# Strassen's product for all three up-projections of a maxout layer, with scan steps and output products placed between its halves

## Chip, cores and metric

One core of a Trainium2 chip. The metric is the device time of one execution in microseconds (us), as the median of several executions. TensorE does the matmuls, VectorE (DVE) and ScalarE (ACT) the work on their results, GpSimd (POOL) helps, SyncE (SP) issues transfers.

## The reference, cut to what matters

A chunked scan (Mamba-2) over 4 sequences of 768 tokens gives x of shape 3072 x 256. A feed-forward layer of the kind "maximum of three" follows, all in fp32:

```python
h = np.maximum(np.maximum(x @ w1, x @ w2), x @ w3)   # 256 -> 768, three times
return (h @ w_out).astype(np.float32)                # 768 -> 256
```

The kernels work on six blocks of 512 tokens. While TensorE does the products of block c, the scan of block c+1 goes on in pieces: transposes (trB, trC), scores (s), state (A) and outputs (y).

## The kernel before

It uses Strassen's product (seven products of half size for eight, in the variant with fewer sums) for w1 alone, from block two on. w2 and w3 go by plain products of 512 columns. A round for two of the six column tiles of w1 has four early products, three VectorE sums that hang on each other, and three late products that add to the same PSUM banks:

```python
def early(c, q):
    A, B = (ps.tile([P, 2, HB], FP32, tag=tag, bufs=1, name=tag) for tag in SUMS)
    quarter_sums(c, q, [(1, A, 0), (6, A, 1), (5, B, 0), (7, B, 1)], True)
    ...
    nc.scalar.copy(out=eu[:, 0], in_=A[:, 0])
    nc.vector.tensor_tensor(out=eu[:, 1], in0=A[:, 1], in1=eu[:, 0], op=ALU.add)
    nc.vector.tensor_tensor(out=v[:, 0], in0=B[:, 1], in1=eu[:, 1], op=ALU.add)
    nc.vector.tensor_tensor(out=parts[:, 3], in0=B[:, 0], in1=v[:, 0], op=ALU.add)

def late(c, q):
    ...
    quarter_sums(c, q, [(2, A, 0), (3, B, 0), (4, B, 1)], False)
```

Between early and late lie long plain products, and the scan steps come with their VectorE work at once:

```python
def scores(n, b):
    scan_weights(n, b, scan_scores(n, b))        # 8 small matmuls, then 4 products on VectorE
...
for q in range(NQ):
    m = late(c, q)
    if n < NC:
        (lambda: transposed(n), lambda: scores(n, 0), lambda: scores(n, 2))[q]()
    ...
    for i in range(1, 3):
        for g in range(2):
            if i == 2 and g == 1 and q + 1 < NQ:
                early(c, q + 1)
            p = group(c, i, 2 * q + g)           # plain product, 512 columns
            ...                                  # running maximum on VectorE
```

At the end of block one stand, in VectorE's order: the last score weights, the state, four sums of w1's quarters, and only then the last step that decodes the third part of wo (`sign()`).

## Time and profile before

| | before |
|---|---|
| median time, us | 319.42 |
| span of the profiled run, us | 318.6 |
| TensorE busy | 94% |
| VectorE busy | 47% |
| length of a steady block, us | 47.3 |
| TensorE idle at the scores, all six blocks, us | 2.9 |

The prediction below shows the engine shares, the clock row, a steady block and the end of block one. This group is what the case turns on; it is the scores' line in the table of the costliest groups (line, engine, operation, count, busy us, mean ns, then TensorE's idle time just before these instructions and what ended it):

```profile
L467 PE MATMUL s<-CT,BT 32*128 32x256 f32 x192 | 14.9, 399 | 2.9 <-ACT CT L417 2.9
```

TensorE hardly waits here, and only twice, for ScalarE's CT before block two (1.36 and 1.55 us).

### The profile page before, as it was taken

Reading aid. Unit: us, or ns where it says so; the run is one execution under the profiler, and the core shown is the slowest. Engines: PE = TensorE matmul, PEld = TensorE weight load, DVE = VectorE, ACT = ScalarE, POOL = GpSimd, SP = SyncE. Lnnn points to the kernel's source line nnn. Section 1 sums busy time; section 2 is a strip of 40 time slices with the busy share of each in tenths; the row PEclk is TensorE's granted clock in tenths of the full one; section 3 lists DMA queues with packets and bytes.
Section 4 is the critical chain, followed back from the end, with each engine's and each line's share of the span. In section 5 each row is a group of like instructions: output and inputs, shape, how many; then the busy total and the mean of one; then the engine's idle time right before and its main releaser. Section 6 shows DMA issues by size and latency. Waiting matters only on the chain.

```text
span 318.6 us, 4707 instructions
## 1 busy us (share of the span) xinstructions
PE 300.0 (94%) x1836; PEld 193.1 (61%) x1836; DVE 150.9 (47%) x268; ACT 108.3 (34%) x281; POOL 55.3 (17%) x58
## 2 busy tenths in 40 slices
PE   6879998659999999999999999999999999999995
PEld 4633443347866548865548865648865658855574
DVE  2597773990336560346460347560347551344410
ACT  2857369510465050460150560241560002100000
POOL 5134563572000600000700000600000000000000
PEclk9999999976999999999999999999999999999999
DMA  7995999891069900077900088701000001000001
GB/s 88 240 387 168 186 249 164 203 120 21 29 189 175 99 0 27 9 209 149 107 2 33 2 232 142 89 0 35 0 34 3 0 0 35 30 5 0 0 0 66
DMA packets 105014, 28.09 MB, mean 88 GB/s; under 512 B 75296, under 2 KB 101920, under 8 KB 104992
## 3 DMA queue, kind: packets, MB, share of 16 engines
q1 hardware_dynamic: 104688, 27.66, 42.1%
q8 instruction: 14, 0.23, 0.3%
q10 hardware_dynamic: 304, 0.13, 0.1%
q14 instruction: 8, 0.07, 0.1%
HBM read 24.54 MB, written 3.24 MB: 87 GB/s over the span
## 4 chain that ended last, share of the span: by engine, by line
PE 80%; DVE 8%; ACT 5%; POOL 2%; issue 2%; DMA 1%; ACTq 0%; POOLq 0%; DVEq 0%
PE up L533 35%; PE o L621 20%; PE sumB L586 8%; PE sumA L586 6%; PE y L497 3%; PE s L467 3%; ACT L L387 2%; DVE L L476 2%; PE y L489 2%; DVE w_u L173 1%; PE spread L313 1%; ACT w_u L172 1%; POOL w_u L182 1%; POOL L L376 1%; DVE w L185 1%
## 5 line engine op out<-in xcount | busy, mean ns | idle before, releaser
L533 PE MATMUL up<-yT,w 128*128 128x512 f32 x312 | 141.0, 597 | 1.5 <-DVE w L185 1.5
L533 PEld LDWEIGHTS up<-yT,w 128*128 128x128 f32 x312 | 57.5, 190 | 65.7 <-issue 57.1
L621 PE MATMUL o<-wo,h 128*128 128x256 f32 x288 | 69.5, 397 | 3.7 <-DVE wo L185 3.7
L621 PEld LDWEIGHTS o<-wo,h 128*128 128x128 f32 x288 | 56.9, 200 | 15.6 <-DVE wo L185 4.1
L387 ACT ACTIVATE L<-L,ncums 128x128 f32<-128x128 f32 x160 | 49.7, 393 | 12.8 <-POOL L L376 12.8
L627 ACT COPY ob<-o 128x512 f32<-128x512 f32 x12 | 7.0, 585 | 77.4 <-PE o L621 77.4
L747 DVE TENSOR_TENSOR h<-m,up 128x512 f32<-128x512 f32 x30 | 20.6, 688 | 26.5 <-PE up L533 26.5
L476 DVE TENSOR_TENSOR L<-s,L 128x512 f32<-128x512 f32 x48 | 29.7, 683 | 3.5 <-PE s L467 3.5
L747 DVE TENSOR_TENSOR m<-m,up 128x512 f32<-128x512 f32 x30 | 20.5, 685 | 21.9 <-PE up L533 21.9
L601 ACT COPY halves<-sumA 128x256 f32<-128x256 f32 x15 | 5.6, 372 | 61.3 <-PE sumA L586 61.3
L511 DVE TENSOR_TENSOR rb<-y,yT 128x256 f32<-128x256 f32 x10 | 4.2, 420 | 41.4 <-ACT yT L502 41.4
L182 POOL TENSOR_TENSOR w_u<-w_u,w_r 128x512 uint32<-128x512 uint32 x12 | 18.1, 1507 | 31.2 <-DVE w_u L176 27.2
L376 POOL TENSOR_SCALAR_AFFINE_SELECT L<-L 128x1024 f32<-128x1024 f32 x20 | 22.8, 1167 | 0.0
L611 DVE TENSOR_TENSOR m<-sumB,halves 128x512 f32<-128x512 f32 x15 | 10.4, 692 | 20.5 <-PE sumB L586 20.5
L586 PE MATMUL sumA<-yT,w 128*128 128x256 f32 x60 | 17.8, 379 | 0.0
L467 PE MATMUL s<-CT,BT 32*128 32x256 f32 x192 | 14.9, 399 | 2.9 <-ACT CT L417 2.9
L586 PEld LDWEIGHTS sumA<-yT,w 128*128 128x128 f32 x60 | 11.4, 190 | 10.1 <-issue 7.2
L453 POOL TENSOR_TENSOR old<-S,E 128x256 f32<-128x256 f32 x4 | 2.5, 618 | 77.3 <-issue 77.3
L586 PE MATMUL sumB<-rb 128*128 128x256 f32 x60 | 15.4, 379 | 0.0
L497 PE MATMUL y<-L,raw_x 128*32 128x128 f32 x384 | 13.7, 275 | 1.2 <-DVE L L476 1.1
L467 PEld LDWEIGHTS s<-CT,BT 32*128 32x128 f32 x192 | 9.5, 184 | 8.3 <-ACT CT L417 4.0
L602 DVE TENSOR_TENSOR halves<-sumA,halves 128x256 f32<-128x256 f32 x15 | 6.4, 425 | 16.5 <-ACT halves L601 16.5
(89 smaller groups left out, 242.3 us busy)
## 6 DMA issues: line engine op xcount, KB each, us to landing
L<-cums SPq DMA_DIRECT2D x10, 1024.0 KB, 9.6
rb<-in_moe_w_dram SPq DMA_DIRECT2D x9, 512.0 KB, 7.7
raw_x<-in_x_dram SPq DMA_DIRECT2D x6, 512.0 KB, 7.7
out_dram<-ob SPq DMA_DIRECT2D x12, 256.0 KB, 2.3
raw_B<-in_B_dram SPq DMA_DIRECT2D x6, 256.0 KB, 4.4
raw_C<-in_C_dram SPq DMA_DIRECT2D x6, 256.0 KB, 6.5
rb<-in_moe_w_out_dram SPq DMA_DIRECT2D x3, 512.0 KB, 5.3
E<-cums SPq DMA_DIRECT2D x40, 32.0 KB, 3.8
```

Of the source, the lines that this page charges most:

```text
L182: nc.gpsimd.tensor_tensor(out=u, in0=u, in1=r, op=ALU.add)
L376: nc.gpsimd.affine_select(out=Ls[c][:, b], in_=Ls[c][:, b], pattern=[[0, NH], [1, P]], compare_op=ALU.is_ge, fill=MASKED, base=0, channel_ ...
L387: nc.scalar.activation(L[:, b, h], L[:, b, h], AF.Exp, bias=ncum[c][:, b * NH + h:b * NH + h + 1], scale=1.0)
L467: nc.tensor.matmul(out=banks[r][:, i].rearrange("j g i -> j (g i)"), lhsT=st["BT"][rows, b], rhs=st["CT"][rows, b].rearrange("p g i -> p ( ...
L476: nc.vector.tensor_tensor(out=M, in0=banks[r], in1=M, op=ALU.mult)
L497: nc.tensor.matmul(out=ys[t][q * D:(q + 1) * D, b], lhsT=st["x"][:, b * NH + h], rhs=M[:, b, h], start=(c == 0 and b == 0), stop=True, til ...
L533: nc.tensor.matmul(out=p, lhsT=w_sb[i][:, k, f * P:(f + 1) * P], rhs=yT[c][:, k], start=(k == 0), stop=(k == KD - 1))
L586: nc.tensor.matmul(out=bank[:, half], lhsT=left(k, q), rhs=sides[c][k], start=(first and half == 0), stop=True, skip_group_check=True)
L611: nc.vector.tensor_tensor(out=parts[:, 1:3], in0=B, in1=eu[:, 1:2].to_broadcast([P, 2, HB]), op=ALU.add)
L621: nc.tensor.matmul(out=o[:, i], lhsT=hT[c][:, f, b * P:(b + 1) * P], rhs=wo_sb[:, f], start=(f == 0), stop=(f == NF - 1), skip_group_check ...
L627: nc.scalar.copy(out=ob, in_=o)
L747: nc.vector.tensor_tensor(out=m[:, g] if i == 1 else h[:, 2 * q + g], in0=m[:, g], in1=p, op=ALU.max)
```

## The change

Intent: w2 and w3 go by Strassen too, which takes 2.5 us of TensorE work from each of five blocks. With no long plain products left to fill the time between early and late products, scan steps and output products of the last block are put there, a few matmuls at a time. A block has now nine rounds (0 to 8). Score weights and maxima go to a list, `later`, from which a few are taken in each round. The diff, cut to its core:

```diff
+    later = []
+    def pop(n): ...                       # issues the first n of the list on VectorE
     def early(c, k):
-        A, B = (ps.tile(..., tag=tag, bufs=1, name=tag) for tag in SUMS)
+        A, B = (sum_bank(kind, [P, 2, HB]) for kind in "AB")      # B has two banks
...
     def late(c, k):
+        products(c, k, [(2, A, 0), (3, B, 0), (4, B, 1)], False)
+        ...                               # maximum with A's half, sum of B and eu
+        pop(1)
+        if i > 0:
+            later.insert(0, lambda: nc.vector.tensor_tensor(
+                out=to[:, 1:4], in0=m[:, 1:4], in1=t, op=ALU.max))
...
     def scores(n, b):
-        scan_weights(n, b, scan_scores(n, b))
+        for r, s in enumerate(scan_scores(n, b)):
+            later.append(lambda r=r, s=s: scan_weight(n, b, r, s))
...                                        # end of block one
+    s23 = scan_scores(1, 2)
+    sign()                                # wo whole before the score weights
+    scan_weights(1, 2, s23)
+    weight_sums(0)                        # on GpSimd now
...
+        for k in range(NW):               # nine rounds
+            early(c, k)
+            ...
+            pop(2)
+            if n < NC and k in (0, 1, 3, 7):
+                ...                       # transposes; scores (1 and 3); half of y
+            elif n < NC or k < NW - 1:
+                if c > 1 or k % 2 == 0:
+                    down_next()           # three output matmuls
+            late(c, k)
+            if n < NC:
+                if k == 0:
+                    ...
+                    later.append(lambda: scan_cd(n))
+                if k < 3 and c > 1:
+                    down_next()
+                ...                       # 4: state, 5 and 6: y, 7: sums of y
```

More of the change, by code (lines that the diff above doesn't have):

```diff
@@ L73, with bank, sum_bank @@
     ctx.enter_context(tc.manual_schedule())
-    SUMS = ("sumA", "sumB")
+    shared = [True]
     turn = {"att": 0, "ffn": 0}
-    shared = [True]
-    def bank_of(kind, n, spare, shape, name):
-        tag = kind
-        if shared[0]:
-            turn[kind] += 1
-            if turn[kind] % (n + 1) == 0:
-                tag = spare
-        return ps.tile(shape, FP32, tag=tag, bufs=n if tag == kind else 1, name=name)
+    def bank(tag, n, shape, name):
+        return ps.tile(shape, FP32, tag=tag, bufs=n, name=name)
+    def sum_bank(kind, shape):
+        return bank("sum" + kind, {"A": 1, "B": 2}[kind], shape, "sum" + kind)
     def att_bank(shape, name):
-        return bank_of("att", 4, SUMS[0], shape, name)
+        turn["att"] += 1
+        if shared[0] and turn["att"] % 5 == 0:
+            return bank("sumA", 1, shape, name)
+        return bank("att", 4, shape, name)
     def ffn_bank(shape, name):
-        return bank_of("ffn", 2, SUMS[1], shape, name)
+        turn["ffn"] += 1
+        if shared[0] and turn["ffn"] % 3:
+            return bank("sumB", 2, shape, name)
+        return bank("ffn", 1, shape, name)
     a_rows = a.rearrange("b h s -> (b h) s")
@@ L394, with scan_b @@
     sides = {}
-    def scan_b(c, bank):
+    def scan_b(c, kind):
         st = blocks[c]
-        tr = bank([HN, NB, P], "trB")
+        tr = kind([HN, NB, P], "trB")
         transposes(tr, st["B"])
@@ L408, in transposes, with scan_tc, scan_c @@
                 identity=ident)
-    def scan_c(c, bank):
+    def scan_tc(c, kind):
         st = blocks[c]
-        tr = bank([HN, NB, P], "trC")
+        st["trC"] = tr = kind([HN, NB, P], "trC")
         transposes(tr, st["C"])
+    def scan_c(c):
+        st = blocks[c]
+        tr = st["trC"]
         st["CT"] = CT = att.tile([HN, NB, 2, P], FP32, tag="CT", name="CT")
@@ L417, in scan_c, with scan_e @@
             nc.scalar.mul(CT[:, :, g], tr, parity[:, g:g + 1])
-        st["trC"] = tr
+    def scan_e(c):
+        E = blocks[c]["E"]
+        nc.scalar.activation(E, E, AF.Exp)
     def scan_cd(c):
@@ L423, in scan_cd @@
         E = st["E"]
-        nc.scalar.activation(E, E, AF.Exp)
         st["Cd"] = Cd = att.tile([HN, NB, P], FP32, tag="Cd", name="Cd")
@@ L471, in scan_scores, with scan_weight, scan_old, scan_own @@
         return banks
+    def scan_weight(c, b0, r, s):
+        M = Ls[c][:, b0:b0 + 2, 2 * r:2 * r + 2]
+        nc.vector.tensor_tensor(out=M, in0=s, in1=M, op=ALU.mult)
     def scan_weights(c, b0, banks):
         for r in range(NP):
-            M = Ls[c][:, b0:b0 + 2, 2 * r:2 * r + 2]
-            nc.vector.tensor_tensor(out=M, in0=banks[r], in1=M, op=ALU.mult)
-    def scan_out(c):
+            scan_weight(c, b0, r, banks[r])
+    def scan_old(c):
+        st = blocks[c]
+        st["y"] = ys = [att_bank([P, NB, P], "y") for _ in range(KD)]
+        if c == 0:
+            return
+        Sp = states[c]
+        for b in range(NB):
+            for r in range(NP):
+                rows = slice(r * PN, (r + 1) * PN)
+                q = r % 2 * 2 * D
+                nc.tensor.matmul(
+                    out=ys[r // 2][q:q + 2 * D, b],
+                    lhsT=Sp[rows, b].rearrange("p g d -> p (g d)"), rhs=st["Cd"][rows, b],
+                    start=(b == 0), stop=False, tile_position=(r * PN, q),
+                    skip_group_check=True)
+    def scan_own(c, bs):
         st = blocks[c]
         M = Ls[c]
-        yT[c] = ffn.tile([P, KD, BLK], FP32, tag="yT", name="yT")
-        ys = [att_bank([P, NB, P], "y") for _ in range(KD)]
-        if c > 0:
-            Sp = states[c]
-            for b in range(NB):
-                for r in range(NP):
-                    rows = slice(r * PN, (r + 1) * PN)
-                    q = r % 2 * 2 * D
-                    nc.tensor.matmul(
-                        out=ys[r // 2][q:q + 2 * D, b],
-                        lhsT=Sp[rows, b].rearrange("p g d -> p (g d)"), rhs=st["Cd"][rows, b],
-                        start=(b == 0), stop=False, tile_position=(r * PN, q),
-                        skip_group_check=True)
-        for b in range(NB):
+        for b in bs:
             for h in range(NH):
@@ L497, in scan_out, with scan_y, scan_sums @@
                 nc.tensor.matmul(
-                    out=ys[t][q * D:(q + 1) * D, b], lhsT=st["x"][:, b * NH + h],
+                    out=st["y"][t][q * D:(q + 1) * D, b], lhsT=st["x"][:, b * NH + h],
                     rhs=M[:, b, h], start=(c == 0 and b == 0), stop=True,
                     tile_position=(0, q * D), skip_group_check=True)
+    def scan_y(c):
+        yT[c] = ffn.tile([P, KD, BLK], FP32, tag="yT", name="yT")
         for t in range(KD):
-            nc.scalar.copy(out=yT[c][:, t], in_=ys[t].rearrange("p b i -> p (b i)"))
-        if c > 0:
-            y11, y12, y21, y22 = (
-                yT[c][:, k, r * HB:(r + 1) * HB] for k in range(2) for r in range(2))
-            late = [ys[k].rearrange("p b i -> p (b i)")[:, r * HB:(r + 1) * HB]
-                    for k in range(2) for r in range(2)]
-            t = kilos([P, 4, HB])
-            for k, (a1, a0) in enumerate((
-                    (late[1], y11), (late[3], t[:, 0]), (late[3], y12), (late[2], t[:, 1]))):
-                nc.vector.tensor_tensor(out=t[:, k], in0=a1, in1=a0, op=ALU.subtract)
-            sides[c] = {1: y11, 2: y21, 3: y22, 4: t[:, 3], 5: t[:, 0], 6: t[:, 1], 7: t[:, 2]}
+            nc.scalar.copy(out=yT[c][:, t], in_=blocks[c]["y"][t].rearrange("p b i -> p (b i)"))
+    def scan_sums(c):
+        y11, y12, y21, y22 = (
+            yT[c][:, k, r * HB:(r + 1) * HB] for k in range(2) for r in range(2))
+        late = [blocks[c]["y"][k].rearrange("p b i -> p (b i)")[:, r * HB:(r + 1) * HB]
+                for k in range(2) for r in range(2)]
+        t = ysum[c % 2]
+        for k, (a1, a0) in enumerate((
+                (late[1], y11), (late[3], t[:, 0]), (late[3], y12), (late[2], t[:, 1]))):
+            nc.vector.tensor_tensor(out=t[:, k], in0=a1, in1=a0, op=ALU.subtract)
+        sides[c] = {1: y11, 2: y21, 3: y22, 4: t[:, 3], 5: t[:, 0], 6: t[:, 1], 7: t[:, 2]}
     hT = {}
@@ L548, in up, with kilos @@
             fill()
-    def kilos(shape):
+    NW = 3 * NQ
+    ysum, quarters, wsum = [], [], {}
+    def kilos(b):
         t = wraw.tile([P, 2, WCOL, 2], U32, tag="rb", name="rb").bitcast(FP32)
-        return t.rearrange("p k f w -> p (k f w)").rearrange(
-            "p (a b) -> p a b", b=shape[-1])[:, 0:shape[1]]
-    wsum = []
-    def weight_sums():
-        a11, a12, a21, a22 = (
-            w_sb[0][:, k].rearrange("p (q g f) -> p g q f", g=2, f=P)[:, g]
-            for g in range(2) for k in range(2))
-        for _ in range(2):
-            t = kilos([P, 2 * NQ, P])
-            wsum.extend([t[:, 0:NQ], t[:, NQ:2 * NQ]])
-        s1, s2, s3, s4 = wsum
-        nc.vector.tensor_tensor(out=s1, in0=a21, in1=a22, op=ALU.add)
-        nc.vector.tensor_tensor(out=s3, in0=a11, in1=a21, op=ALU.subtract)
-        nc.vector.tensor_tensor(out=s2, in0=s1, in1=a11, op=ALU.subtract)
-        nc.vector.tensor_tensor(out=s4, in0=a12, in1=s2, op=ALU.subtract)
@@ L577, in left, with places @@
-    def left(k, q):
-        if k in (1, 2, 4):
-            g, row = {1: (0, 0), 2: (0, 1), 4: (1, 1)}[k]
+        return t.rearrange("p k f w -> p (k f w)").rearrange("p (a b) -> p a b", b=b)
+    def places():
+        for _ in range((NW + 1) // 2):
+            t = kilos(P)
+            for half in (t[:, 0:4], t[:, 4:8]):
+                if len(wsum) < NW:
+                    wsum[len(wsum)] = half
+        ysum.extend(kilos(HB) for _ in range(2))
+        quarters.extend(kilos(HB)[:, 0:3] for _ in range(2))
@@ new lines, in weight_sums @@
+    def weight_sums(k):
+        q, i = divmod(k, 3)
+        a11, a12, a21, a22 = (
+            w_sb[i][:, kk, (2 * q + g) * P:(2 * q + g + 1) * P]
+            for g in range(2) for kk in range(2))
+        s1, s2, s3, s4 = (wsum[k][:, j] for j in range(4))
+        nc.gpsimd.tensor_tensor(out=s1, in0=a21, in1=a22, op=ALU.add)
+        nc.gpsimd.tensor_tensor(out=s3, in0=a11, in1=a21, op=ALU.subtract)
+        nc.gpsimd.tensor_tensor(out=s2, in0=s1, in1=a11, op=ALU.subtract)
+        nc.gpsimd.tensor_tensor(out=s4, in0=a12, in1=s2, op=ALU.subtract)
@@ L580, in left, with products @@
+    def left(p, k):
+        if p in (1, 2, 4):
+            q, i = divmod(k, 3)
+            g, row = {1: (0, 0), 2: (0, 1), 4: (1, 1)}[p]
             f = 2 * q + g
-            return w_sb[0][:, row, f * P:(f + 1) * P]
-        return wsum[{5: 0, 6: 1, 7: 2, 3: 3}[k]][:, q]
-    def quarter_sums(c, q, products, first):
-        for k, bank, half in products:
+            return w_sb[i][:, row, f * P:(f + 1) * P]
+        return wsum[k][:, {5: 0, 6: 1, 7: 2, 3: 3}[p]]
+    def products(c, k, which, first):
+        for p, bank, half in which:
@@ L586, in quarter_sums @@
             nc.tensor.matmul(
-                out=bank[:, half], lhsT=left(k, q), rhs=sides[c][k],
+                out=bank[:, half], lhsT=left(p, k), rhs=sides[c][p],
                 start=(first and half == 0), stop=True, skip_group_check=True)
-    open_ = {}
-    def half_tile():
-        return wtmp.tile([P, 2, HB], FP32, tag="w_u", name="halves")
-    def early(c, q):
-        A, B = (ps.tile([P, 2, HB], FP32, tag=tag, bufs=1, name=tag) for tag in SUMS)
-        quarter_sums(c, q, [(1, A, 0), (6, A, 1), (5, B, 0), (7, B, 1)], True)
-        m = maxima_tile()
-        parts = m.rearrange("p g (r t) -> p (g r) t", r=2)
-        eu, v = half_tile(), half_tile()
+    later = []
@@ new lines, in pop, with early @@
+    def pop(n):
+        while n and later:
+            later.pop(0)()
+            n -= 1
+    held = {}
+    def early(c, k):
+        q, i = divmod(k, 3)
+        A, B = (sum_bank(kind, [P, 2, HB]) for kind in "AB")
+        products(c, k, [(1, A, 0), (6, A, 1), (5, B, 0), (7, B, 1)], True)
+        if i == 0:
+            held["m"] = ffn.tile([P, 4, HB], FP32, tag="m", name="m")
+        t = held["m"][:, 1:4] if i == 0 else quarters[k % 2]
+        eu = wtmp.tile([P, 2, HB], FP32, tag="w_u", name="eu")
+        v = wtmp.tile([P, 2, HB], FP32, tag="w_r", name="v")[:, 0]
@@ L601, in early @@
         nc.scalar.copy(out=eu[:, 0], in_=A[:, 0])
         nc.vector.tensor_tensor(out=eu[:, 1], in0=A[:, 1], in1=eu[:, 0], op=ALU.add)
-        nc.vector.tensor_tensor(out=v[:, 0], in0=B[:, 1], in1=eu[:, 1], op=ALU.add)
-        nc.vector.tensor_tensor(out=parts[:, 3], in0=B[:, 0], in1=v[:, 0], op=ALU.add)
-        open_[c, q] = A, B, eu, m, parts
-    def late(c, q):
-        A, B, eu, m, parts = open_.pop((c, q))
-        quarter_sums(c, q, [(2, A, 0), (3, B, 0), (4, B, 1)], False)
-        nc.scalar.copy(out=parts[:, 0], in_=A[:, 0])
-        nc.vector.tensor_tensor(
-            out=parts[:, 1:3], in0=B, in1=eu[:, 1:2].to_broadcast([P, 2, HB]), op=ALU.add)
-        return m
@@ L615, in down @@
-    def down(c, u, between=None):
-        o = ffn_bank([P, 2, DM], "o")
-        for i in range(2):
-            b = 2 * u + i
-            fill()
-            for f in range(NF):
-                nc.tensor.matmul(
-                    out=o[:, i], lhsT=hT[c][:, f, b * P:(b + 1) * P], rhs=wo_sb[:, f],
-                    start=(f == 0), stop=(f == NF - 1), skip_group_check=True)
-            if i == 0 and between:
-                between()
-        ob = ffn.tile([P, 2, DM], FP32, tag="ob", bufs=3, name="ob")
-        nc.scalar.copy(out=ob, in_=o)
-        nc.sync.dma_start(
-            out=out.rearrange("(b s) m -> s b m", s=S)[c * P:(c + 1) * P, 2 * u:2 * u + 2],
-            in_=ob)
+        nc.vector.tensor_tensor(out=v, in0=B[:, 1], in1=eu[:, 1], op=ALU.add)
@@ new lines, in early, with late @@
+        nc.vector.tensor_tensor(out=t[:, 2], in0=B[:, 0], in1=v, op=ALU.add)
+        held["open"] = A, B, eu, t
+    def late(c, k):
+        q, i = divmod(k, 3)
+        m = held["m"]
+        A, B, eu, t = held.pop("open")
+        products(c, k, [(2, A, 0), (3, B, 0), (4, B, 1)], False)
+        to = h_of(c)[:, 2 * q:2 * q + 2].rearrange(
+            "p g (r t) -> p (g r) t", r=2) if i == 2 else m
+        if i == 0:
+            nc.scalar.copy(out=m[:, 0], in_=A[:, 0])
+        else:
+            nc.vector.tensor_tensor(out=to[:, 0], in0=m[:, 0], in1=A[:, 0], op=ALU.max)
+        nc.vector.tensor_tensor(
+            out=t[:, 0:2], in0=B, in1=eu[:, 1:2].to_broadcast([P, 2, HB]), op=ALU.add)
+        pop(1)
+        if i > 0:
+            later.insert(0, lambda: nc.vector.tensor_tensor(
+                out=to[:, 1:4], in0=m[:, 1:4], in1=t, op=ALU.max))
@@ new lines, with down_next @@
+    downs = []
+    def down_next(kind=ffn_bank):
+        if not downs:
+            return
+        c, j = downs.pop(0)
+        u, i, half = j // 4, j // 2 % 2, j % 2
+        if j % 4 == 0:
+            held["o"] = kind([P, 2, DM], "o")
+        o = held["o"]
+        b = 2 * u + i
+        for f in range(half * NQ, (half + 1) * NQ):
+            nc.tensor.matmul(
+                out=o[:, i], lhsT=hT[c][:, f, b * P:(b + 1) * P], rhs=wo_sb[:, f],
+                start=(f == 0), stop=(f == NF - 1), skip_group_check=True)
+        if j % 4 == 3:
+            ob = ffn.tile([P, 2, DM], FP32, tag="ob", bufs=3, name="ob")
+            nc.scalar.copy(out=ob, in_=o)
+            nc.sync.dma_start(
+                out=out.rearrange("(b s) m -> s b m", s=S)[c * P:(c + 1) * P, 2 * u:2 * u + 2],
+                in_=ob)
@@ L649 @@
     first_sums(3)
-    scan_c(0, ffn_bank)
+    scan_tc(0, ffn_bank)
+    scan_c(0)
     decode()
@@ L660 @@
     decode()
-    scan_out(0)
+    scan_old(0)
+    scan_own(0, range(NB))
+    scan_y(0)
     for _ in range(6):
@@ L675, with decay_list, part @@
     load(1, "x")
-    def decays_of(c):
-        if c >= NC:
-            return []
-        return [lambda b=b, g=g: decay_part(c, b, g) for b in range(NB) for g in range(2)]
+    def decay_list(c):
+        return [(c, b, g) for b in range(NB) for g in range(2)]
+    parts = {c: decay_list(c) for c in range(1, NC)}
+    def part(c):
+        if parts.get(c):
+            decay_part(*parts[c].pop(0))
     def first_tokens():
@@ L688, in first_tokens @@
             ncum[c], from_j[c] = ncums[:, :, c], from_js[:, :, c]
-    pieces = [(up, f) for f in range(NF)] + [(down, u) for u in range(NB // 2)]
-    d = decays_of(1)
+    d = [lambda p=p: decay_part(*p) for p in parts.pop(1)]
     nothing = lambda: None
@@ L702, in loads @@
             load(c, "x")
-            fillers.append(lambda: decay_mask(c, 0))
-            fillers.extend(decays_of(c))
     def transposed(n):
         scan_b(n, att_bank)
-        scan_c(n, att_bank)
+        scan_tc(n, att_bank)
         if n < NC - 1:
@@ L721 @@
             transposed(1)
+            scan_c(1)
         if f == 4:
+            scan_e(1)
             scan_cd(1)
-            scores(1, 0)
+            scan_weights(1, 0, scan_scores(1, 0))
             loads(2)
-        if f == 5:
-            shared[0] = False
-            scores(1, 2)
-            scan_state(1)
-            weight_sums()
-    for c in range(NC):
-        n = c + 1
-        if c > 0:
-            for q in range(NQ):
-                m = late(c, q)
-                if n < NC:
-                    (lambda: transposed(n), lambda: scores(n, 0), lambda: scores(n, 2))[q]()
-                if q == 2:
-                    loads(c + 2)
-                h = h_of(c)
-                for i in range(1, 3):
-                    for g in range(2):
-                        if i == 2 and g == 1 and q + 1 < NQ:
-                            early(c, q + 1)
-                        p = group(c, i, 2 * q + g)
-                        nc.vector.tensor_tensor(
-                            out=m[:, g] if i == 1 else h[:, 2 * q + g], in0=m[:, g], in1=p,
-                            op=ALU.max)
-                        if (i, g) != (1, 1):
-                            fill()
-                        elif n < NC and q == 0:
-                            scan_cd(n)
-                        elif n < NC - 1 and q == 1:
-                            scan_state(n)
-        for u in range(2):
-            sign()
-            if u == 0:
-                down(c, 0)
-                if n < NC:
-                    scan_out(n)
-            else:
-                down(c, 1, (lambda: early(n, 0)) if n < NC else None)
@@ new lines @@
+    shared[0] = False
+    s23 = scan_scores(1, 2)
+    sign()
+    scan_weights(1, 2, s23)
+    places()
+    weight_sums(0)
+    decay_mask(2, 0)
+    downs += [(0, j) for j in range(8)]
+    down_next()
+    down_next()
+    scan_state(1)
+    part(2)
+    down_next()
+    part(2)
+    down_next()
+    scan_old(1)
+    scan_own(1, range(NB))
+    scan_y(1)
+    part(2)
+    scan_sums(1)
+    weight_sums(1)
+    down_next()
+    for c in range(1, NC):
+        n = c + 1
+        for k in range(NW):
+            early(c, k)
+            if k < 4:
+                for _ in range((1, 2, 1, 1)[k] if c == 1 else min(k, 1)):
+                    part(n)
+            else:
+                part(n + 1)
+            pop(2)
+            if n < NC and k in (0, 1, 3, 7):
+                if k == 0:
+                    transposed(n)
+                elif k == 7:
+                    scan_own(n, (2, 3))
+                    scan_y(n)
+                else:
+                    scores(n, k - 1)
+            elif n < NC or k < NW - 1:
+                if c > 1 or k % 2 == 0:
+                    down_next()
+            late(c, k)
+            if c == 1 and k + 2 < NW:
+                weight_sums(k + 2)
+            if n < NC:
+                if k == 0:
+                    loads(c + 2)
+                    scan_c(n)
+                    scan_e(n)
+                    later.append(lambda: scan_cd(n))
+                if k < 3 and c > 1:
+                    down_next()
+                elif k == 3 and n + 1 < NC:
+                    decay_mask(n + 1, 0)
+                elif k == 4 and n < NC - 1:
+                    scan_state(n)
+                elif k == 5:
+                    scan_old(n)
+                elif k == 6:
+                    pop(9)
+                    scan_own(n, (0, 1))
+                elif k == 7:
+                    scan_sums(n)
+        pop(9)
+        while downs:
+            down_next()
+        downs += [(c, j) for j in range(8)]
@@ L767 @@
+    while downs:
+        down_next(att_bank)
 _INS = ['x', 'a', 'B', 'C', 'moe_w1', 'moe_w2', 'moe_w3', 'moe_w_out']
```

## The prediction

> **What bounds the kernel now.** I read the page's engine shares and clock row first, then the groups, then the chain that ended last, then busy time by block, then the timeline around one round of Strassen products.
>
> ```profile
> PE 300.0 (94%) x1836; PEld 193.1 (61%) x1836; DVE 150.9 (47%) x268; ACT 108.3 (34%) x281; POOL 55.3 (17%) x58
> PEclk9999999976999999999999999999999999999999
> ```
>
> TensorE is busy 94% of 318.6 us, and its clock is full except in two slices near 64 to 80 us. Busy time by engine for the second block of tokens:
>
> ```profile
> 87.97:135.31 47.34, 47.34 (x307) 31.19 (x307) 21.40 (x38) 19.50 (x58) 6.58 (x7) 1.00 0.45 84
> ```
>
> Columns: stretch, length, then busy us of PE, PEld, DVE, ACT, POOL, clock. In a steady block TensorE never idles; VectorE works 21.4 of 47.3 us. So TensorE work removed there is time removed, until VectorE, from which TensorE waits for sums, becomes the bound. The other place that matters is the end of block one, in the chain (start, length, what):
>
> ```profile
> 62.32 0.68 DVE h L546
> 63.00 2.40 DVE L L476 x4
> 65.40 0.33 DVE S L448
> 65.73 0.47 DVE rb L572
> 66.20 1.00 DVE rb L573
> 67.19 1.37 DVE rb L574
> 68.59 1.33 DVE rb L575
> 69.91 1.51 DVE wo L185
> 71.47 6.48 PE o L621 x16
> ```
>
> Here VectorE holds the chain: the score weights, the four weight sums (rb), then the last third of wo, for which the output products wait. TensorE idles 2.65 us before 63.66 and 3.74 us before 71.47, and its clock falls:
>
> ```profile
> 64.00:65.00 1.00, 1.00 (x29) 0.83 (x22) 1.00 (x3) 0.00 (x0) 0.11 (x1) 0.50 1.37 129
> 68.00:69.00 1.00, 0.00 (x0) 0.00 (x0) 0.96 (x2) 0.82 (x3) 1.00 (x2) 1.00 0.40 35
> 73.00:74.00 1.00, 1.00 (x4) 0.82 (x3) 0.00 (x0) 0.00 (x0) 0.40 (x1) 0.50 0.00 0
> ```
>
> The third column from the end is the clock: 0.50 at 64 to 65 and 73 to 74. One round of Strassen products, with its chain:
>
> ```profile
> 83.49 0.59 PE L586 MATMUL sumA<-yT,w 128*128 128x256 f32 x2
> 84.55 0.37 ACT L601 COPY halves<-sumA 128x256 f32<-128x256 f32 x1 [1.52 <-PE sumA L586]
> 84.96 0.42 DVE L602 TENSOR_TENSOR halves<-sumA,halves 128x256 f32<-128x256 f32 x1 [1.93 <-ACT halves L601]
> 85.48 0.42 DVE L603 TENSOR_TENSOR halves<-sumB,halves 128x256 f32<-128x256 f32 x1
> 85.94 0.42 DVE L604 TENSOR_TENSOR m<-sumB,halves 128x256 f32<-128x256 f32 x1
> ```
>
> The early four products start at 83.49 and end 1.72 us later; the third sum ends at 86.36, 2.87 us after that start. Whatever VectorE does next in order cannot start before about +2.8.
>
> **What the Trainium skill says.** "TensorE: Matmul & The Clock Gate", Part 3, "What overlaps and what doesn't": matmuls start and end strictly in order; only weight loads are pulled ahead. So one waiting matmul holds all behind it; the 3.74 us gap agrees. Same page, Part 1: an idle window of about 3.4 us halves the clock. The trace has it at 0.50 already after gaps of 2.65 and 3.74 us, for 3.2 and 6.8 us. "GPSIMD Engine Reference", section 8, Key points: GpSimd shares SBUF interfaces with VectorE instructions of two SBUF inputs. The trace agrees: of the four 128x384 sums the first took 549 ns, the others, beside busy POOL, 1080 to 1435. "VectorE: DVE Perf Modes", Mode 1x: an fp32 sum of two tensors makes one result a cycle; 425 ns for 256 and 685 for 512 columns agree.
>
> **The change, part by part.** A 512-column matmul (two records) takes 0.859 us (six in 5.15), a 256-column one 0.4315.
>
> (1) Work. w2 and w3 too go by Strassen: per block 24 matmuls of 0.859 (20.61 us) become 42 of 0.4315 (18.12). Five blocks: -12.4 us, all on TensorE's path.
>
> (2) Switches. After every step on array tiles (scores, state, y) the next full matmul starts 0.19 us late: 7.06 against 6.87 us for the same 16 records, after scores and without. Scan steps cut into six pieces instead of four: 2 x 0.19 x 4 blocks = +1.5 us.
>
> (3) The end of block one. The weight sums move to POOL and the last sign step of wo comes ahead of the score weights. POOL's last decode add ends at 63.53, so wo is whole at about 64.3. From 61.0 TensorE does two output matmuls, waits for wo's second third (62.4), two more, waits until 64.35 (idle 1.65 in all, in two pieces, so no throttling), then two, the state (0.6), six (2.6), y (2.9 and a switch), three (1.3). Round 0 of block two then starts at about 73.1 instead of 83.5: -10.4. It has done 15 instead of 18 output matmuls (+1.3). Net -9 us.
>
> (4) VectorE. The 60 maxima of 685 ns go. A round is three sums of 425, one of 690, and in two rounds of three a maximum of 425 and one of 768 columns (two SBUF inputs; 150 + 768/0.96 = 950 ns, an estimate from the rows above, free of POOL). Nine rounds: 3 x 1.97 + 6 x 3.34 = 26 us, plus 8.3 of scan steps: 34 of some 48 us, against 21. It is not full, but it is in order, and the new order makes TensorE wait. From the built program's semaphore waits:
>
> Round 1: the first four score banks. The fourth is the bank of trC, and waits for Cd, which stands on VectorE behind that round's three sums. Cd runs from +2.8 to +3.5 us; TensorE has been ready for it at about +2.1. After it come five small matmuls (0.68 us) and a switch, so the late products start at +4.4 instead of +3.0: 1.4 us, in block two 2.0, as ScalarE's copy comes behind CT and E. Four blocks: 6 us.
>
> Round 3: the second four score banks are the first four again; the last waits for the fourth score weight, behind the three sums (+2.87), the 768-column maximum (to +3.75) and itself (to +4.35). Late products at +5.3 instead of +3.0: 2.3 us, in block two, with POOL at the weight sums beside a maximum that may take 2.3 us, some 3. Four blocks: 10 us.
>
> Round 8: the four y sums (5.0 to 6.5 us after the start of round 7) delay that round's chain, and its maximum the next block's first product: 0.6 us, three blocks; 1.9 in block two, which has no output product there. Sum 3.7.
>
> Block two's rounds 2 and 5, which have no output products after or between: about 1.5. Block six's last round: 1.0, no product between.
>
> Where TensorE resumes after a semaphore its weight load (190 ns) isn't ahead: some 8 times, +1.5 us.
>
> Sum of waits: 6 + 10 + 3.7 + 1.5 + 1.0 + 1.5 = 23.7; I take 22.5, as some overlap. Net: -12.4 + 1.5 - 9 + 22.5 = +2.6, so 318.9 becomes about 321.5. A steady block would be about 50 us, of which 45.3 is work (27.2 products, 10.4 output, 6.5 scan, 1.2 switches), against 47.3.
>
> **Rivals.** A: the waits are hidden and the change pays in full: -12.4 + 1.5 - 9 = -20, 299 us. For it: 24 pieces were evidently placed to cover the chain, and in rounds 4 to 7 they do (late products at +3.0, sums done at +2.87). Against it: in rounds 1 and 3 the waited-for instruction is behind the chain by order, not by speed. B: the waits also throttle the clock. TensorE would idle some 2.3 us in round 3 (longer in block two); gaps of 2.65 and 3.74 did it, one of 1.36 at 12 us did not. A cold window of 3.4 us costs 1.7; in half the blocks that is +3 to +7: 325 to 329. C: VectorE becomes the bound in block two, where POOL's 36 sums slow all its two-SBUF maxima (6 x up to 1.3 us): +5 at most, as block two has just 39 us of TensorE work. D: the end of block one gives nothing, as the yT copies on ScalarE stand behind eight decays that wait for a POOL mask, now behind weight sums: then +9, 330.
>
> **Range and chances.** The gains of (1) and (3) are the surer terms, about -21; the waits could be from 12 (311) to 31 (330). I predict 321, range 311 to 330. Faster by over 2% (below 312.5) needs the waits under 13.5 us, which the order of VectorE speaks against: 0.16. Slower by over 2% (above 325.3) needs rival B or C: 0.28. Within 2%: 0.56.
>
> **What would show it.** Right: the first sumA product of block two near 73 us; blocks three to five about 50 us each with PE busy near 45; the largest PE waits at the scores (on Cd and on L, the score weights), about 1.4 and 2.3 us each; VectorE busy 34 us in a block. Wrong: steady blocks near 45 to 46 with no PE waits at the scores (rival A), a clock under 1.00 in steady blocks (B), or 768-column maxima above 1.5 us (C).

## The result, and the profile after

The changed kernel takes 333.44 us (332.61 to 336.44, 4 runs) against 319.42 (317.72 to 320.17) of the kernel before: ratio 1.046, 95% interval 1.039 to 1.054. A ratio is the mean time of one kernel's fast runs over that of the other's of the same rounds, so it is not quite the ratio of the medians quoted. The kernel is slower, above the predicted range, and the forecast (321, most likely within 2%) was wrong.

The kernel after: engine shares and clock row from its page, and the scores' group from the fuller table of groups by shape, which names more than one releaser.

```profile
PE 302.5 (91%) x2016; PEld 228.0 (69%) x2016; DVE 200.4 (60%) x384; ACT 120.2 (36%) x311; POOL 72.5 (22%) x94
PEclk9999999999979999978999997999999999999999
L476 PE MATMUL s<-CT,BT 32*128 32x256 f32 x192 | 21.4, 427 | 15.5 <-DVE L L484 7.7 <-DVE Cd L435 4.9 <-ACT CT L424 2.9
```

TensorE waits 12.6 us more at the scores: 7.7 for score weights (L) and 4.9 for Cd, both on VectorE. It is "busy" longer (302.5 against 300.0 us) although it has less to do: three stretches of 3.41, 6.83 and 3.41 us ran at clock 0.50, where matmuls take longer. The scores' mean rose from 399 to 427 ns, about half of it for that reason: without such stretches it is 412 (run 4). The clock row has new dips in four slices. Blocks two, three and five, in busy time by engine:

```profile
73.07:121.80 48.73, 43.47 (x314) 33.11 (x312) 31.35 (x63) 20.71 (x62) 20.79 (x36) 0.96 0.49 101
121.80:176.28 54.48, 50.88 (x343) 40.30 (x343) 32.52 (x63) 18.45 (x52) 7.39 (x7) 0.94 0.29 47
228.61:278.82 50.21, 46.82 (x310) 37.62 (x310) 31.76 (x62) 12.54 (x32) 0.00 (x0) 1.00 0.03 11
```

Block two starts at 73.07 us, 10.4 earlier than before (83.49). But a block then takes 50.2 us where the clock is full (block five, clock 1.00) and 54.5 where it is not (block three, 0.94), against 47.3. VectorE is busy some 32 us of 50: not full.

Round 3 of block three, in the timeline (start, us, engine, line, operation):

```profile
140.66 0.59 PE L616 MATMUL sumA<-yT,w 128*128 128x256 f32 x2
142.18 0.42 DVE L640 TENSOR_TENSOR eu<-sumA,eu 128x256 f32<-128x256 f32 x1 [1.20 <-ACT eu L639]
142.49 0.71 PE L476 MATMUL s<-CT,BT 32*128 32x256 f32 x6
142.71 0.42 DVE L641 TENSOR_TENSOR v<-sumB,eu 128x256 f32<-128x256 f32 x1
143.17 0.42 DVE L642 TENSOR_TENSOR m<-sumB,v 128x256 f32<-128x256 f32 x1
143.51 0.95 DVE L660 TENSOR_TENSOR h<-m,rb 128x768 f32<-128x768 f32 x1
144.37 0.68 DVE L484 TENSOR_TENSOR L<-s,L 128x512 f32<-128x512 f32 x1
145.11 2.00 PE L476 MATMUL s<-CT,BT 32*128 32x256 f32 x10 [1.92 <-DVE L L484]
147.04 1.22 PE L616 MATMUL sumA<-yT,w 128*128 128x256 f32 x2
```

Read it downwards. The round starts at 140.66. Three of the eight score matmuls (two records each) go at 142.49. The fourth needs the bank that the fourth score weight of round 1 still has to read. That weight (L484) stands on VectorE behind the three sums and the maximum of 768 columns, and ends at 145.05. TensorE idles 1.92 us. The clock then (third column from the end) while TensorE is busy nearly all the time:

```profile
145.00:146.00 1.00, 0.89 (x8) 0.79 (x9) 0.06 (x1) 0.00 (x0) 0.00 (x0) 0.61 0.00 0
146.00:147.00 1.00, 1.00 (x6) 0.33 (x1) 0.00 (x0) 0.00 (x0) 0.00 (x0) 0.50 0.00 0
151.00:152.00 1.00, 1.00 (x4) 0.78 (x3) 0.29 (x1) 0.24 (x1) 0.00 (x0) 0.50 0.00 0
```

It stays at 0.50 for 6.83 us; a matmul of 256 columns starts every 0.86 us instead of 0.43. In round 1 the same pattern has Cd in the place of the weight:

```profile
130.12 0.42 DVE L642 TENSOR_TENSOR rb<-sumB,v 128x256 f32<-128x256 f32 x1
130.49 0.69 DVE L435 TENSOR_TENSOR Cd<-trC,E 128x512 f32<-128x512 f32 x1
131.33 1.10 PE L476 MATMUL s<-CT,BT 32*128 32x256 f32 x10 [1.19 <-DVE Cd L435]
```

Round lengths, from the start of one first sumA product to the next in the timeline (us):

| block | 0 | 1 | 2 | 3 | 4 | 5 | 6 | 7 | 8 | sum |
|---|---|---|---|---|---|---|---|---|---|---|
| two | 3.96 | 6.25 | 4.74 | 7.97 | 5.71 | 5.25 | 5.53 | 4.33 | 4.99 | 48.73 |
| three | 5.81 | 7.44 | 5.61 | 9.10 | 6.13 | 5.54 | 5.53 | 4.33 | 4.99 | 54.48 |
| four | 5.34 | 7.45 | 5.61 | 8.52 | 5.02 | 5.55 | 5.52 | 4.34 | 4.98 | 52.33 |
| five | 5.35 | 7.44 | 5.61 | 6.90 | 4.52 | 5.55 | 5.52 | 4.34 | 4.98 | 50.21 |

Round 3 is the one that differs between blocks: 6.90 at full clock, up to 9.10 where the clock fell behind its wait. In block six, which has no scan, rounds 1 to 7 take 4.31 or 4.32 us each, which is ten matmuls of 0.4315 and no wait.

### The profile page after: what moved, and what is told of

The parts are those of the page before. It is cut to its first block, busy times and chain, and to the rows that moved or that the text cites. A ratio compares the mean times of both kernels' runs of the same rounds, so it can differ in the third digit from the quotient of the medians.

```text
span 331.7 us, 5268 instructions
## 1 busy us (share of the span) xinstructions
PE 302.5 (91%) x2016; PEld 228.0 (69%) x2016; DVE 200.4 (60%) x384; ACT 120.2 (36%) x311; POOL 72.5 (22%) x94
## 4 chain that ended last, share of the span: by engine, by line
PE 66%; DVE 18%; ACT 7%; issue 4%; POOL 3%; DVEq 0%; ACTq 0%; POOLq 0%
PE sumB L616 19%; PE o L676 17%; PE sumA L616 17%; PE s L476 3%; PE y L514 3%; ACT L L390 3%; DVE L L484 2%; DVE v L641 2%; DVE eu L640 2%; DVE rb L532 2%; PE y L501 2%; POOL w_u L185 1%; DVE h L660 1%; DVE rb L656 1%; DVE w_u L176 1%
## 5 line engine op out<-in xcount | busy, mean ns | idle before, releaser
L616 PE MATMUL sumA<-yT,w 128*128 128x256 f32 x180 | 59.1, 411 | 1.6 <-DVE eu L640 0.9
L616 PE MATMUL sumB<-rb 128*128 128x256 f32 x180 | 46.5, 381 | 0.0
L616 PEld LDWEIGHTS sumA<-yT,w 128*128 128x128 f32 x180 | 32.3, 196 | 14.4 <-issue 4.8
L616 PEld LDWEIGHTS sumB<-rb 128*128 128x128 f32 x180 | 34.7, 193 | 4.9
L476 PE MATMUL s<-CT,BT 32*128 32x256 f32 x192 | 21.4, 427 | 15.5 <-DVE L L484 7.7
L554 PE MATMUL up<-yT,w 128*128 128x512 f32 x72 | 32.3, 598 | 1.5 <-DVE w L188 1.5
L484 DVE TENSOR_TENSOR L<-s,L 128x512 f32<-128x512 f32 x48 | 31.3, 682 | 0.0
L616 PE MATMUL sumB<-yT,rb 128*128 128x256 f32 x90 | 29.0, 405 | 1.8 <-DVE rb L642 1.2
L616 PE MATMUL sumB<-rb,w 128*128 128x256 f32 x90 | 28.2, 396 | 0.0
L616 PE MATMUL sumA<-rb 128*128 128x256 f32 x90 | 27.5, 388 | 0.0
L656 DVE TENSOR_TENSOR m<-sumB,eu 128x512 f32<-128x512 f32 x15 | 10.4, 692 | 26.6 <-PE sumB L616 26.6
L554 PEld LDWEIGHTS up<-yT,w 128*128 128x128 f32 x72 | 13.2, 190 | 18.1 <-issue 12.6
L656 DVE TENSOR_TENSOR rb<-sumB,eu 128x512 f32<-128x512 f32 x30 | 20.7, 691 | 7.4 <-PE sumB L616 7.0
L185 POOL TENSOR_TENSOR w_u<-w_u,w_r 128x512 uint32<-128x512 uint32 x12 | 18.1, 1506 | 31.4 <-DVE w_u L179 30.3
```

The lines of the kernel that those rows point to most:

```text
L185: nc.gpsimd.tensor_tensor(out=u, in0=u, in1=r, op=ALU.add)
L476: nc.tensor.matmul(out=banks[r][:, i].rearrange("j g i -> j (g i)"), lhsT=st["BT"][rows, b], rhs=st["CT"][rows, b].rearrange("p g i -> p ( ...
L484: nc.vector.tensor_tensor(out=M, in0=s, in1=M, op=ALU.mult)
L554: nc.tensor.matmul(out=p, lhsT=w_sb[i][:, k, f * P:(f + 1) * P], rhs=yT[c][:, k], start=(k == 0), stop=(k == KD - 1))
L616: nc.tensor.matmul(out=bank[:, half], lhsT=left(p, k), rhs=sides[c][p], start=(first and half == 0), stop=True, skip_group_check=True)
L656: nc.vector.tensor_tensor(out=t[:, 0:2], in0=B, in1=eu[:, 1:2].to_broadcast([P, 2, HB]), op=ALU.add)
```

## The experiments

Theory: TensorE waits in rounds 1 and 3 because what frees the fourth score bank stands behind the round's sums in VectorE's order, and the wait of round 3 halves the clock. Rivals: VectorE is short of time, so that a wait moved comes back elsewhere; the clock falls for another reason; the early start of block two is not worth what it seems. Each kernel is the changed one with the edit shown, except the fifth, and all gave right results. Kernels 1 to 4 ran on one chip, 5 to 7 on another, each beside runs of the kernel before (319.51 us on the first chip, 318.75 on the second).

### 1. Cd ahead of round 1's sums

```diff
-                    later.append(lambda: scan_cd(n))
+                    scan_cd(n)
```

> Only Cd (the product that frees the fourth score bank of round 1) is put on VectorE ahead of that round's three sums. Theory (TensorE waits for an instruction that stands behind the sums in VectorE's order): round 1 of blocks 3 to 5 falls from 7.44 to about 5.6 to 5.8 us, the 1.2 to 1.3 us waits for Cd go, in all 6 to 7.5 us less: about 326.5. Rival (VectorE is short of time, or Strassen's rounds are slow as such): the wait comes back elsewhere in the block and the time moves by less than 2 us.

Measured: 322.70 us (321.50 to 323.31), ratio to the kernel before 1.010 (1.006 to 1.014). Rounds 1 fell from 6.25, 7.44, 7.45 and 7.44 us to 4.63, 5.59, 5.59 and 5.59, and the waits for Cd are gone; no other round took them over. That is 7.2 us, as the theory has it. The rest of the 10.7 us is clock: mean 0.989 against 0.979, two stretches of 3.41 us at 0.50 in place of 13.65 us. Round 1 of block three has all its score matmuls in one piece:

```profile
126.46 1.15 PE L476 MATMUL s<-CT,BT 32*128 32x256 f32 x16
```

The wait of 1.92 us in round 3 is still there in all four blocks, but the clock fell behind it only in blocks three and five ("What stays open" says why): rounds 3 took 7.01, 7.75, 6.90 and 8.12.

### 2. The fourth score weight ahead of round 3's sums

```diff
-        pop(1)
+        pop(2 if k == 2 else 1)
```

> Only the fourth score weight of round 1 is put at the end of round 2 on VectorE instead of behind round 3's sums and maximum. Theory: round 3 falls from 6.9 (8.0 to 9.1 where the clock fell) to about 4.4 us in four blocks, and with the 1.92 us wait go the cold stretches (3.4, 6.8 and 3.4 us at clock 0.50): about 10 us of waits and 6 of clock, 317 to 319. Rival (the cold clock has another cause): about 10 us less, 323.5, and the clock still falls.

Measured: 315.87 us (315.00 to 318.16), ratio 0.988 (0.984 to 0.993): 17.6 us less than the changed kernel, a little below the expected range. Rounds 3 fell to 4.40, 4.30, 4.29 and 4.29. One part of the expectation missed: the clock still fell in the profiled run, twice in the rounds, behind the waits for Cd in blocks two and four. Block four:

```profile
175.25 1.10 PE L476 MATMUL s<-CT,BT 32*128 32x256 f32 x10 [1.19 <-DVE Cd L435]
177.00:178.00 1.00, 1.00 (x4) 0.82 (x3) 0.42 (x1) 0.00 (x0) 0.00 (x0) 0.50 0.49 66
```

The lines are of the timeline and of the table by stretches. Round 1 of that block took 9.13 us; those of blocks three and five, with the same wait, 7.44 and 7.45. In block two, where the wait is 1.29 us, the clock was 0.50 from 81.07 to 84.48, and rounds 1 and 2 took 7.10 and 5.56 us against 6.25 and 4.73. A third such stretch, from 16.21 on, came before the rounds. So an idle gap of 1.2 or 1.3 us can be followed by half clock, some of the time. The profiled run was the slowest of the four (318.16 us, clock 0.984); the other three (315.00 to 316.13) had a mean clock of 1.000.

### 3. Both moves

> Both moves. Theory: the savings add, as the two waits lie in different rounds: 333.4 - 7 - 16 = about 310, steady blocks near 46.5 us, clock mean 0.99 or more. Rival (VectorE short of time): less than two thirds of the sum of e1 and e2.

Measured: 308.47 us (307.71 to 309.08), ratio 0.966 (0.962 to 0.970). The two savings by themselves are 10.7 and 17.6 us, 28.3 together; both moves save 25.0. They add but for the clock: some 3.5 us of it are counted in both. The same round 3 as above, in the timeline:

```profile
133.47 1.15 PE L476 MATMUL s<-CT,BT 32*128 32x256 f32 x16
133.69 0.42 DVE L641 TENSOR_TENSOR v<-sumB,eu 128x256 f32<-128x256 f32 x1
134.15 0.42 DVE L642 TENSOR_TENSOR m<-sumB,v 128x256 f32<-128x256 f32 x1
134.49 0.95 DVE L660 TENSOR_TENSOR h<-m,rb 128x768 f32<-128x768 f32 x1
134.55 0.70 PE L616 MATMUL sumA<-yT,w 128*128 128x256 f32 x2
```

All eight score matmuls go at once, and the late products start at 134.55 while the maximum still runs: VectorE does the same work in the same time, but nothing waits for it. Clock mean 1.000 in the profiled run (0.989 in one of the four). The rival that VectorE is short of time is refuted: it is as busy as before the moves (200 us), and the saved time stayed saved.

### 4. TensorE kept busy during the wait

```diff
         banks = [bank([P, 2, 2, P], "s") for bank in kinds]
+        for _ in range(4 if warm else 0):     # round 3 only; overwritten at once
+            nc.tensor.matmul(
+                out=banks[0][:, 0].rearrange("j g i -> j (g i)"), lhsT=left(1, warm[1]),
+                rhs=sides[warm[0]][1], start=True, stop=True, skip_group_check=True)
```

> The changed kernel with all its waits, but four matmuls of 128x128 on 256 columns, whose results are overwritten at once, stand ahead of the scores of round 3, inside the wait. They take 1.73 us of a wait of 1.92. Theory (that wait is what halves the clock): no stretch at 0.50 after block one, round 3 about 6.9 us in all four blocks, time 6 to 7 us less, about 327. Rival (the clock falls for another reason, or its fall costs little): the same or up to 3 us longer than the changed kernel.

Measured: 326.57 us (325.81 to 327.49), ratio 1.023 (1.019 to 1.027). Sixteen useless matmuls made the changed kernel 6.9 us faster. Clock row, and round 3 of block three in the timeline:

```profile
PEclk9999999999999999999999999999999999999999
140.80 1.89 PE L473 MATMUL s<-yT,w 128*128 128x256 f32 x8
143.52 1.13 PE L480 MATMUL s<-CT,BT 32*128 32x256 f32 x10 [0.19 <-DVE L L488]
```

The late half of the scores still waits for the same weight, so rounds 3 take 7.01, 6.90, 6.90 and 6.90. The wait in itself is untouched; only the idleness is gone, and with it the half clock. So the clock's share of the loss is 6.9 us, and the rival that it falls behind round 3 for another reason is out. (The page is of one execution with mean clock 1.000; one of the four had 0.993, with no trace to say where.)

### 5. The kernel before with the new end of block one alone

```diff
-            scores(1, 2)
-            scan_state(1)
-            weight_sums()
+            s23 = scan_scores(1, 2)
+            sign()
+            scan_weights(1, 2, s23)
...
-                down(c, 0)
+                down(c, 0, (lambda: (scan_state(1), weight_sums())) if c == 0 else None)
```

> The kernel before, with only the new ending of block one: wo's last sign step ahead of the score weights, and the state step and weight sums behind the first six output products. Theory (this ending was worth 9 us of the change by itself): the first Strassen product of block two comes at about 74.4 instead of 83.5 us, no cold clock near 72 us, blocks 47.3 us as before, about 310. Rival (the ending gains only together with the later placing of three output products and of the sums on GpSimd): less than 5 us.

Measured: 311.24 us (310.68 to 311.90), ratio 0.977 (0.975 to 0.979). The timeline at that place:

```profile
64.26 1.13 PE L621 MATMUL o<-wo,h 128*128 128x256 f32 x4 [1.58 <-DVE wo L185]
74.30 0.59 PE L586 MATMUL sumA<-yT,w 128*128 128x256 f32 x2
```

The first Strassen product of block two comes at 74.30 instead of 83.49, 9.2 us earlier, as does the end of the profiled run (309.4 against 318.6), and the clock stays at 1.00 there. The medians differ by 7.5; the profiled run of the kernel before was a slow one (320.36). So the reordering at the end of block one was worth about 7.5 us by itself (9.2 in the profiled pair), and needs neither Strassen for w2 and w3 nor the weight sums on GpSimd.

### 6. Both moves, and two sums of y between the late sums of round 7

The first two of the four sums in `scan_sums` are issued between the two late VectorE instructions of round 7, the others where they were.

> Both moves of VectorE work as in the earlier run, and the first two of the four y sums stand between the two late sums of round 7. Theory (what round 8 loses, 0.66 us, comes from the y sums ending late on VectorE): round 8 falls from 4.98 to about 4.6 us in four blocks, about 1.2 to 1.5 us less than with both moves alone: 307. Rival (round 8 waits for its own maximum anyway): no change, 308.5.

Measured: 306.19 us (306.11 to 306.70), ratio 0.961 (0.959 to 0.964). Round 8 fell from 4.98 to 4.45 or 4.48 us in blocks two to five, a little more than expected. It is the fastest kernel, 3.9% faster than the kernel before. Block three of it, busy time by engine:

```profile
114.04:160.49 46.45, 46.16 (x344) 37.68 (x343) 32.71 (x62) 18.37 (x52) 7.39 (x7) 1.00 0.34 57
```

TensorE is busy 46.2 of 46.5 us, and VectorE 32.7, more than half as much again as the 21.4 of the kernel before.

### 7. VectorE's order as it was, an output product ahead of the scores

```diff
                 else:
+                    if c > 1:
+                        down_next()
                     scores(n, k - 1)
...
-                if k < 3 and c > 1:
+                if (k == 0 or k == 2) and c > 1:
```

The output product of round 4 between early and late is left out as well in blocks three to five, so that each block has as many as before.

> The changed kernel with VectorE's order as it is; in blocks three to five an output product of another round (1, and 4) stands ahead of the scores of rounds 1 and 3, so TensorE reaches the waiting matmul 1.3 us later. Theory (the wait ends at a fixed time set by VectorE): round 1 falls from 7.44 to about 6.15, round 3 stays at 6.9 with one product more in it, round 4 falls from 5.0 to about 4.6, and the waits of some 1 us no longer halve the clock in these blocks: about 323 to 325. Rival (TensorE waits for a bank or weights at the scores and the wait moves with them): no change, 333.

Measured: 323.44 us (322.97 to 323.87), ratio 1.016 (1.013 to 1.019). In blocks three to five rounds 1 took 6.14, 6.15 and 6.15, rounds 3 took 6.90 in all three, with a product more in them, and rounds 4 took 4.63, 4.63 and 4.52; each expected figure was met. Block two, which has no product to spare, still lost the clock (round 3: 8.32). The wait of round 3 of block three, 1.92 us before, in the timeline:

```profile
142.93 1.12 PE L476 MATMUL s<-CT,BT 32*128 32x256 f32 x10 [0.62 <-DVE L L484]
```

It is 1.3 us shorter, by just the output product put ahead of it. So the wait ends at a fixed time that VectorE's order sets. Filling it saves 10.0 us; ending it earlier (3) saves 25.0.

## Why the prediction was wrong

**Right.** The mechanism and nearly all places. Block two was to start at 73.1 and started at 73.07. The waits for Cd in round 1 and for the fourth score weight in round 3 were named, and shown by runs 1 to 3 and 7. Work: rounds without scan take just ten matmuls of 0.4315 us. Rival C failed: of the 30 maxima of 768 columns the median is 950 ns in the trace, and only one took as long as 1409. Five of them ran beside a busy POOL, and took 948, 1006, 1409, 948 and 950 ns. So the prediction's reading that VectorE slows beside a busy POOL was too general (in its own trace the first of the four sums, with 549 ns, also ran 0.3 us beside POOL). VectorE is busy 31.4 to 32.5 us in blocks two, three and five, a little under the 34 predicted. Rival D failed: the decays on ScalarE did not hold the end of block one.

**The step that failed** is the sum at the end of point (4) of the change: "Sum of waits: 6 + 10 + 3.7 + 1.5 + 1.0 + 1.5 = 23.7; I take 22.5, as some overlap." Two terms of it were mis-sized:

- The clock was given nothing in it. The prediction left the half clock to rival B, at +3 to +7, as an addition in the chances. It measured 6.9 us (run 4; in the profiled runs rounds 3 and 4 of blocks two, three and four lose 1.7, 3.3 and 1.7 us to it), and belonged in the central sum: the waits of round 3 were predicted at 2.3 us, near the 2.65 us gap that had already halved the clock in the trace of before.
- The waits do not overlap; they lie in different rounds, and add. From run 4, which has them without the cold clock, blocks two to five last 47.03, 51.19, 50.68 and 50.21 us. Their work by the prediction's own figures is 38.7, 45.2, 45.2 and 44.4 (27.2 products, 3.9 or 10.4 output, 6.5 scan, and switches of six times 0.19, which it rounded to 1.2; block five has no state step and its switch). The waits are then 8.3, 6.0, 5.5 and 5.8; block six adds 1.1 (38.6 us from its first product to the last block's output, less 37.5 of work). Sum 26.7, against 22.5. Round 1 costs 1.85 us more than without its wait (7.44 against 5.59) where 1.4 was predicted, and round 3 2.6 (6.90 against 4.30) where 2.3 was: in four blocks 7.2 and 10.4 us, against 6 and 10.

Together: -12.4 + 1.5 - 9.1 + 26.7 + 6.9 = +13.6 us; the medians differ by 14.0. The forecast's sum was +2.6. Of the 11 us between the two, 6.9 are the clock and 4.2 the waits (26.7 against 22.5; the last tenth is rounding). The switches (+1.5) were not measured by themselves.

A sign of the slip stood in the prediction. Its start at 73.1, some 47 us for block two (38.7 of work and its waits), three blocks of 50, and the 52.9 us that block six and the last outputs took in the trace, give a span of 323 and a time of some 325 us, not 321.5 (an estimate). Adding both ways would have shown about 3 of the 12 us that were missing.

**What stays open.** One question the kept traces do answer: why the same wait of 1.92 us was followed by half clock in blocks two, three and four and not in five (where a stretch starts and ends was read from the trace's clock record itself). In that record every stretch but the last, full or half, is a multiple of 3.413 us (3.41, 6.83, 47.79 and 85.33 in the changed kernel), so the clock changes only at the edges of windows of that length, wherever the kernel then is. The profiled runs of the changed kernel, of run 1 and of run 7 have nine gaps of 1.92 us. Six lay with at least 1.83 us inside one window, in which TensorE was then busy 44 to 46%; each was followed by 0.50. Three were cut by an edge into parts of at most 1.54 us, and the clock stayed full. Block five's gap, from 249.54 to 251.46 with an edge at 251.03, is one of these:

```profile
251.46 1.13 PE L476 MATMUL s<-CT,BT 32*128 32x256 f32 x10 [1.92 <-DVE L L484]
```

So part of this loss is luck of position.

Open is what went on in run 2: the two windows before its falls in the rounds were busy 62 and 65%, while one of 65% in its block three (around the gap at 125.98) left the clock full. All three held mostly scores, on 32 of the array's 128 rows; whether such matmuls count for less was not tested. Open, too, is why the clock of block three stayed at 0.50 for a second window, though TensorE was busy all through the first. The first round of block three takes 5.81 us where those of four and five take 5.35; in the trace it follows the one maximum of 1409 ns (at 122.56, beside POOL), behind which that round's sums stand. Run 6 was compared with run 3 over different chips; that it is better rests on its round 8 and on the two ratios, whose intervals just overlap.

## What to carry to other kernels

When long matmuls that hid a chain on another engine are taken away, list for each matmul put into the gap which instruction frees its bank, and where that stands in the other engine's order: here two instructions that had no reason to be behind the chain turned a loss of 4.6% into a gain of 3.4%. A wait of TensorE that stands in the plan costs more than its length, since behind about 2 us of idleness the clock may halve for 3 to 7 us; count it in the sum, not among the risks. And measure parts of a change by themselves: the reordering at the end of block one paid 2.3% alone, and was hidden under the rest. What the other parts add to it, once most of the waits are mended, is 5.0 us (run 6 against run 5, on one chip), and not the 12.4 us of work that Strassen takes away.

## What the Trainium skill lacked or had wrong

- "TensorE: Matmul & The Clock Gate", Why this matters for your kernels, advises no TensorE gaps over about 3 us to keep the clock. Here gaps of 1.92 us were followed by a clock of 0.50 for 3.4 or 6.8 us in three blocks of four, and in run 2 gaps of 1.29 and 1.19 us in two blocks of four; the measurement decides. All nine gaps of 1.92 us fit one reading: at least 1.83 us idle in one window of 3.41 us and the clock halved, at most 1.54 and it did not.
- "TensorEngine Tiling (Array Packing)", Key Properties, has that a change of tiling mode drains TensorE, but not what it costs. A full matmul behind a step on array tiles starts 0.19 us late here (7.06 against 6.87 us for the same 16 records, kernel before).
- No page read says that waits inside a kernel can be filled with matmuls whose result is thrown away, to hold the clock: 16 of them gained 6.9 us (run 4).
- "GPSIMD Engine Reference", section 8, gives no size for the contention with VectorE: five maxima of two SBUF inputs beside a busy POOL took 948, 948, 950, 1006 and 1409 ns, against 948 to 959 for the other 25 (kernel after).
